# The end stage of an adaLN attention block: casts and dQ matmuls in other places, fp32 gradient tiles from GpSimd, transposes' buffers at 512 B

## The chip, the core and the metric

The kernel runs on one core of a Trainium2 chip. The metric is the device time of one execution in microseconds, the median of several runs. A profile is one further view: one execution, recorded by the hardware profiler. Below, PE is TensorE, DVE is VectorE, ACT is ScalarE, POOL is GpSimd and SP is SyncE, which here only issues DMAs.

## The reference

One transformer block with adaptive layer norm, forward and backward, with S = 2048 tokens, D = 512 features, H = 32 heads of 16, F = 1792 hidden units, all inputs in bf16:

```python
mod = silu(c) @ w_mod            # six rows: sa, ca, ga, sb, cb, gb
h  = layernorm(x) * (1 + ca) + sa
x1 = x + ga * (softmax_attention(h @ wqkv) @ wo)
h2 = layernorm(x1) * (1 + cb) + sb
y  = x1 + gb * (relu(h2 @ w1 + b1)**2 @ w2 + b2)
out, vjp = jax.vjp(block, x, wqkv, wo, w1, b1, w2, b2, c, w_mod)
return (out, *vjp(grad_out))
```

The outputs are y and the gradients of x, wqkv, wo, w1, b1, w2, b2, c and w_mod (`out_0` to `out_9`).

## The kernel before

The work runs in stages. In brackets stands the time of each stage in the profiled run before.

1. **Forward attention with the MLP in its shadow** (0 to 981 us). Queries go in four chunks of 512 tokens. ACT's exponentials (L385) set the pace. Projections, layer norms and the MLP of earlier chunks are background generators that are advanced between the attention's pieces (`bg.step`, `bg.until`, `bg.take`).
2. **The last chunk** (`last_chunk`, L743, about 982 to 1055). The attention's pools are closed, and the last 512 tokens go through the output projection `wo`, the second layer norm, the MLP and its backward. Here `gT` is the transposed slice of `grad_out`, fetched by a transposing DMA from SP (L776). It is the right-hand side of `du_mm` (L794), whose first groups are computed ahead between the four token tiles of the output projection (L800). Each such tile is added to x by DVE (L801, `x1_l`), normalised, and written as `xh`; turns of `xh` on PE (L763) feed the MLP's first layer (L821).
3. **dW1 and dW2** (`gen_dw1`, L927, and `gen_dw2`; about 1055 to 1169). dW1 goes block by block over 14 slices of 128 hidden units. Each slice needs `du_blk`, a transposing DMA from DRAM issued by SP, two slices ahead, and a `w1_blk` from POOL. PE multiplies (L964), and DVE finishes the gradient and two sums over it into a scrap tile `junk`.
4. **The attention's backward** (`attn_bwd`, L1364; about 1169 to 2450). Scores and exponentials are computed again, DVE forms the score gradients `ds` (L1438), and `ds` is needed twice: as it is for dK and dV, and transposed for dQ. Most of the transposing is done by DMAs (`dsT`, L1446, 256 of them, issued by SP), the rest by turns on PE. `dq` (L1412) adds 32 matmuls of a group to the accumulator `accq`; its finished chunk goes by DVE to `dq_t`, the token-major gradient of Q. `dk_t` and `dv_t` are the same for K and V. Crossbar buffers here are the SBUF tiles that the transposing DMAs read or write: `ds`, `dsT`, `du_blk`, `a_blk`, `dqT`, `dq_t`, `dk_t`, `dv_t`.
5. **The tail of the backward and the end stage** (`attn_bwd`'s last lines and `phase6`, L1572; about 2434 to 2567). The gradient of wqkv is a product per part `t` (0 for Q, 1 for K, 2 for V) and row block `kt`: `dw_mm` is 16 matmuls on PE (3.5 us), `dw_end` two steps on ACT and DVE and a store by POOL. Three of these products (`k0`, `v0`, `k1`) and the column sums (`col_sum`, `cs_bc`) start in the backward's tail; the other nine are `dw(t, kt)`.

The end stage is a list of such steps, written out by hand:

- `dx(st)`, for each of 16 token tiles: 12 matmuls over `dqT`, the transposed gradients of Q, K and V (PE, L1638); an eviction by ACT (L1643); the layer norm's backward on DVE (L1654, L1656); `cast(st)`, which writes the tile's fp32 residual gradient as bf16 into `dx1b` (ACT, L1676); ACT adds a term to the fp32 tile `gp` (L1652); a store by POOL.
- `load_a(i)`, for each pair of token tiles, three pairs ahead: three transposing DMAs into `dqT` and two loads of fp32 residual gradients into `dx1_6`, all from SP.
- `dwo(nt)`: 16 matmuls over `dx1b`, one for each token tile (L1681), the gradient of `wo`.
- `mod(j)`, for each of the six rows: one matmul, a copy and four scalings on ACT (L1707) into `dwm7`, a tile with one buffer, a 512 KB store by POOL (L1708), and four dots on DVE.
- `diag`, `dsa`, `load_wmod`, `load_wo`, `load_o`: small steps and loads for the above (the loads from POOL).

Order: PE, SP and, in the backward's core, POOL follow the order of the program; in the backward's tail and in `phase6` all engines do. Elsewhere a scheduler may reorder ACT, DVE and POOL. Tiles are placed in SBUF by pools, one behind the other, so that a tile's start follows from the sizes of those ahead of it.

Of the kernel before, what the change touches and what calls it, by code (L numbers as in the profile page):

```python
# [9 lines left out]
BF16 = mybir.dt.bfloat16  # L10
F32 = mybir.dt.float32
# [8 lines left out]
P = 128  # L20
# [85 lines left out]
class K:  # L106
# [160 lines left out]
    def phase_fwd(self):  # L267
# [9 lines left out]
        self.dgb_acc = pp.tile([P, D], F32, name="dgb_acc")  # L277
        self.csq = pp.tile([P, D], F32, name="csq")
        self.dc_part = pp.tile([P, DT, 6], F32, name="dc_part")
        self.dsb_col = pp.tile([P, DT], F32, name="dsb_col")  # L280
        self.dcb_col = pp.tile([P, DT], F32, name="dcb_col")
        self.db1 = pp.tile([P, FT], F32, name="db1")
# [80 lines left out]
        for n, (qc, g, jp) in list(enumerate(order))[2:]:  # L363
# [36 lines left out]
            if jp == 1 and n + 1 < len(order):  # L400
                if n < 2 * NQ - 1:
                    bg.until(-(g + 1))
                KT = KTn
        bg.until(f"fc2_{SC - 2}")
        x0s = []
        for k in range(2):
            t = self.mk.tile([P, D], BF16, name="x0", bufs=2)
# [335 lines left out]
    def last_chunk(self, bg, O_b, x0s):  # L743
# [27 lines left out]
        g_tm = e0.tile([P, ST, D], BF16, name="g_tm")  # L771
        xh2 = e0.tile([P, ST, D], BF16, name="xh2")
        gt4, xh = g_tm[:, st0:, :], xh2[:, st0:, :]
        OT = mk.tile([P, 4, DT, P], BF16, name="fT", bufs=2)
        gT = mk.tile([P, DT, 512], BF16, name="fT", bufs=2)
        nc.sync.dma_start_transpose(gT[:], io["grad_out"][0, s0:s0 + 512, :])  # L776
        nc.sync.dma_start(gt4, tm_v(io["grad_out"][0]))
        nc.sync.dma_start(xh2[:, :st0, :], self.xhat2_d.rearrange("(st p) d -> p st d", p=P)[:, :st0, :])
        nc.sync.dma_start(g_tm[:, :st0, :], io["grad_out"][0].rearrange("(st p) d -> p st d", p=P)[:, :st0, :])
# [147 lines left out]
    def gen_dw1(self, sb, xh2):  # L927
        nc, io = self.nc, self.io
        D, F, ST, DT, FT = self.D, self.F, self.ST, self.DT, self.FT
        db1 = self.db1  # L930
        w1_v = io["B_w1"].rearrange("(kt p) f -> p kt f", p=P)
        dw1_v = io["out_4"].rearrange("(kt p) f -> p kt f", p=P)
        dcb_part = sb.tile([P, DT, FT], F32, name="dcb_part", bufs=1)
        dsb_part = sb.tile([P, DT, FT], F32, name="dsb_part", bufs=1)
        db1_row = sb.tile([1, F], BF16, name="db1_row", bufs=1)
        nc.vector.memset(dcb_part[:], 0.0)
        nc.vector.memset(dsb_part[:], 0.0)
        blks = []

        def load(ft):  # L940
            r = sb.tile([P, ST, P], BF16, name="du_blk", bufs=3)
            cuts = (0, ST - 4, ST) if ft < 2 else (0, ST)
            for (a, b) in zip(cuts, cuts[1:]):
                nc.sync.dma_start_transpose(r[:, a:b, :], self.duT_d[ft, :, a * P:b * P])
            w = sb.tile([P, DT, P], BF16, name="w1_blk", bufs=3)
            with nc.allow_non_contiguous_dma(reason="256B runs"):
                nc.gpsimd.dma_start(w[:], w1_v[:, :, ft * P:(ft + 1) * P])
            diag = sb.tile([P, P], F32, name="diag", bufs=3)
            nc.gpsimd.tensor_scalar(diag[:], self.ident_f[:], db1[:, ft:ft + 1], 1.0, ALU.mult, ALU.mult)
            blks.append((r, w, diag))  # L950

        for ft in range(2):
            load(ft)
        yield 0
        for ft in range(FT):
            if ft + 2 < FT:
                load(ft + 2)
            else:
                yield ("dw1", 0)
            du, w1_blk, diag = blks[ft]  # L960
            g4 = self.dps.tile([P, DT, P], F32, name="dps")
            for kt in range(DT):
# [12 lines left out]
            for kt in range(DT):  # L975
                nc.scalar.activation(t1[:, kt, :], csb[:], ACT.Copy, scale=self.mod_col(3)[:, kt:kt + 1])
                nc.vector.scalar_tensor_tensor(dw1[:, kt, :], g4[:, kt, :], self.opcbT[:, kt:kt + 1], t1[:, kt, :], ALU.mult, ALU.add)
                junk = sb.tile([P, P], F32, name="junk")
                nc.vector.scalar_tensor_tensor(junk[:], g4[:, kt, :], 1.0, w1_blk[:, kt, :], ALU.mult, ALU.mult,
                                               accum_out=dcb_part[:, kt, ft:ft + 1])  # L980
                junk2 = sb.tile([P, P], F32, name="junk")
                nc.vector.scalar_tensor_tensor(junk2[:], csb[:], 1.0, w1_blk[:, kt, :], ALU.mult, ALU.mult,
                                               accum_out=dsb_part[:, kt, ft:ft + 1])
            with nc.allow_non_contiguous_dma(reason="256B runs"):
                nc.gpsimd.dma_start(dw1_v[:, :, ft * P:(ft + 1) * P], dw1[:])
        nc.gpsimd.dma_start(io["out_5"].rearrange("(o f) -> o f", o=1), db1_row[:])
        nc.vector.tensor_reduce(self.dcb_col[:], dcb_part[:], axis=AX.X, op=ALU.add)
        nc.vector.tensor_reduce(self.dsb_col[:], dsb_part[:], axis=AX.X, op=ALU.add)
# [286 lines left out]
    def phase5(self):  # L1275
# [6 lines left out]
        self.dv_t = opa.tile([P, ST, D], BF16, name="dv_t")  # L1282
        self.opa = opa
        self.junk6 = opa.tile([P, D], F32, name="junk6")
        self.dsa_part = opa.tile([P, DT, 3], F32, name="dsa_part")
        nc.gpsimd.memset(self.dsa_part[:], 0.0)
        nc.gpsimd.memset(self.dc_part[:], 0.0)
        assert ST * self.H == D
# [10 lines left out]
    def open_bwd(self):  # L1299

        nc = self.nc
        S, ST, D, DT = self.S, self.ST, self.D, self.DT
        xp = self.open_pool("p5x", bufs=1, side="right")
        self.wp = self.open_pool("p5w", bufs=1, side="right")
        cp = self.open_pool("p5c", bufs=1, side="right")
# [1 line left out]
        self.q0 = xp.tile([P, 2 * S + 3 * ST * 4 * DH], BF16, name="q0")  # L1307
        self.xhat1_6 = m01[:, :ST * D].rearrange("p (st d) -> p st d", d=D)
        self.wq_6 = self.q0[:, :3 * DT * D].rearrange("p (kt n) -> p kt n", n=3 * D)
        self.kvs = cp.tile([P, 1], F32, name="kvs")  # L1310
        nc.vector.memset(self.kvs[0:64], self.scale)
        nc.vector.memset(self.kvs[64:P], 1.0)
        m23 = cp.tile([P, 4 * S], BF16, name="m23")
# [50 lines left out]
    def attn_bwd(self):  # L1364
# [9 lines left out]
        G = 4  # L1374
# [81 lines left out]
            nc.scalar.copy(dsT[:, 0:4, :], tp[:])  # L1456
            grp.append(dsT)

        tick = kvp.tile([1, 1], BF16, name="tick")
        T = self.T0  # L1460
        turnq, last = [], None
        for g in range(NQ):
# [50 lines left out]
        with tc.manual_schedule(engines=ALL):  # L1513
# [12 lines left out]
            k0, v0, k1 = [dpp.tile([P, 512], F32, name="dp") for _ in range(3)]  # L1526
            self.dw_mm(k0, 1, 0, 0, ST // 2)
            turn(*turnq.pop(0))
            for _ in range(G):
                dq(pendq.pop(0), [0, 1])  # L1530
            self.dw_mm(v0, 2, 0, 0, ST // 2)
            self.dw_mm(k0, 1, 0, ST // 2, ST)
            self.col_sum(1)
            self.dw_mm(v0, 2, 0, ST // 2, ST)
            self.col_sum(2)
            self.cs_bc(1)
            while pendq:
                dq(pendq.pop(0), [0, 1])
            self.cs_bc(2)
            self.dw_mm(k1, 1, 1, 0, ST)  # L1540
        assert not turnq and not pend
        self.dw_open = [(1, 0, k0), (2, 0, v0), (1, 1, k1)]

# [28 lines left out]
    def phase6(self):  # L1572
# [45 lines left out]
        def load_a(i):  # L1618
            s2 = 2 * i
            dqT = wk.tile([P, 3, 2, DT, P], BF16, name="dqT", bufs=3)  # L1620
            for t in (1, 2, 0):
                nc.sync.dma_start_transpose(dqT[:, t].rearrange("p s n k -> p (s n) k"),
                                            parts[t][:, s2:s2 + 2, :].rearrange("p s d -> p (s d)"))
            dx1s = [wk.tile([P, D], F32, name="dx1_6", bufs=6) for _ in range(2)]
            for k in range(2):
                nc.sync.dma_start(dx1s[k][:], dx1_v[:, s2 + k, :])
            nxt[i] = (dqT, dx1s)

        for i in range(2):
# [85 lines left out]
        diag(3, self.dsb_col)  # L1715
        diag(4, self.dcb_col)
        dw(1, 2, stp, "st")
        dsa(1)
        self.col_sum(0)
        load_a(2)  # L1720
        dw(1, 3, dpp, "dp")
        dsa(2)
# [2 lines left out]
        dx1b = sb.tile([P, ST, D], BF16, name="dx1b")  # L1725
        O_tm = sb.tile([P, ST, D], BF16, name="O_tm")
        dga = dgs[2] = sb.tile([P, D], F32, name="dga_acc")
        dx(0)
        dw(2, 1, dpp, "dp")
        mod(3)  # L1730
        dx(1)
        load_wmod(4)
        dw(2, 2, dpp, "dp")
        dx(2)
        load_wmod(0)
        dw(2, 3, dpp, "dp")
        mod(4)
        dx(3)
        load_o(0)
        dw(0, 0, dpp, "dp")  # L1740
        dx(4)
        load_wmod(1)
        dw(0, 1, dpp, "dp")
        load_o(1)
        dsa(0)
        dx(5)
        dw(0, 2, dpp, "dp")
        load_o(2)
        dx(6)
        dw(0, 3, dpp, "dp")  # L1750
        nc.vector.tensor_reduce(dsa_col[:], dsa_part[:], axis=AX.X, op=ALU.add)
        nc.vector.tensor_reduce(dca_col[:], dca_part[:], axis=AX.X, op=ALU.add)
        load_o(3)
        dx(7)
        diag(0, dsa_col)
        diag(1, dca_col)
        load_wo(0)
        load_wo(1)
        dx(8)
        mod(0)  # L1760
        dx(9)
        mod(1)
        dx(10)
        load_wmod(2)
        dx(11)
        for st in range(12, ST):
            cast(st)
        dwo(0)
        dx(12)
        load_wo(2)  # L1770
        dwo(1)
        dx(13)
        load_wo(3)
        dwo(2)
        dwo(3)
        dx(14)
# [83 lines left out]
```

## Time and profile before

| | us |
|---|---|
| median of 5 runs | 2571.58 |
| the five runs | 2568.52, 2571.07, 2571.58, 2574.01, 2574.53 |
| profiled execution, its own time | 2568.52 |
| its span in the profile | 2566.7 |
| PE busy in the span | 2467.2 (96%) |
| ACT busy | 2313.4 (90%) |
| DVE busy | 1762.0 (69%) |
| POOL busy | 559.5 (22%) |
| DMA bytes, mean rate | 432.18 MB, 168 GB/s |

The profiled execution is the fastest of the five runs. Its span is 1.8 us shorter than its time. The mean granted clock of TensorE was 0.994 of full speed. Busy shares are means over the stages named above, which have different limits. In lines of the chain of waits the two numbers are the start and the length of a piece; in lines of the timeline they are the start and the duration of a group of like instructions, and the bracket at the end is the idle time of the engine before it and what ended that. A line number refers to the kernel before.

### The profile page before, as it was taken

How to read it: one execution, taken by the hardware profiler on the slowest of the kernel's cores; microseconds unless marked ns; L12 is line 12 of the kernel's file. 1: busy time of each engine (PE TensorE's matmuls, PEld its weight loads, DVE VectorE, ACT ScalarE, POOL GpSimd, SP SyncE). 2: the span in 40 equal slices, each digit the busy share in tenths (PEclk: the TensorE clock that was granted, in tenths of full speed). 3: DMA queues.
4: the chain of work that ended last, by engine and by line, in shares of the span. 5: the costliest groups of instructions: out<-in, count | busy, mean ns of one | idle time of the engine just before them, and what ended most of it. 6: DMA issues, size and time to landing. Idle time of an engine off the chain costs nothing.

```text
span 2566.7 us, 77585 instructions
## 1 busy us (share of the span) xinstructions
PE 2467.2 (96%) x31011; PEld 1223.9 (48%) x31239; DVE 1762.0 (69%) x3651; ACT 2313.4 (90%) x3761; POOL 559.5 (22%) x1113
## 2 busy tenths in 40 slices
PE   8999899999999998999999999999999999999997
PEld 4555555555555554663444444444444444444443
DVE  6222223423322344667999999999999999999976
ACT  7999999999999996416999999999999999999954
POOL 3454521320221131452111111111111111101122
PEclk9999999999999999999999999999999999999999
DMA  4598752450451154999999999999999999999995
GB/s 165 117 177 199 174 93 86 108 111 22 118 129 49 46 139 117 237 216 207 204 202 201 200 200 201 199 205 199 201 201 200 203 205 198 198 199 203 226 224 157
DMA packets 1196032, 432.18 MB, mean 168 GB/s; under 512 B 1137604, under 2 KB 1163078, under 8 KB 1195670
## 3 DMA queue, kind: packets, MB, share of 16 engines
q1 hardware_dynamic: 1158342, 324.75, 65.4%
q0 software_dynamic: 37328, 102.47, 13.3%
q8 instruction: 244, 4.00, 0.6%
q14 instruction: 118, 0.97, 0.1%
HBM read 74.26 MB, written 68.69 MB: 56 GB/s over the span
## 4 chain that ended last, share of the span: by engine, by line
PE 60%; ACT 28%; DMA 5%; issue 5%; DVE 1%; POOL 0%; SPq 0%; ACTq 0%; POOLq 0%; DVEq 0%
ACT pu L385 24%; PE st L1497 19%; PE acckv L1390 10%; PE accq L1412 8%; PE st L382 4%; PE dp L1436 3%; ACT pu L1501 2%; DMA dsT<-ds 2%; PE st L1455 2%; PE dps L1015 2%; PE accbank L316 2%; PE dps L964 1%; PE dp L1546 1%; PE st L1638 1%; PE pps L1176 1%
## 5 line engine op out<-in xcount | busy, mean ns | idle before, releaser
L1438 DVE TENSOR_TENSOR ds<-dp,pu 128x512 bf16<-128x512 f32 x2048 | 1237.1, 682 | 18.1 <-PE dp L1436 11.1
L1501 ACT ACTIVATE pu<-st 128x512 bf16<-128x512 f32 x2048 | 1074.0, 612 | 77.6 <-PE st L1497 50.8
L385 ACT ACTIVATE pu<-st 128x1024 bf16<-128x1024 f32 x992 | 912.0, 1077 | 5.0 <-PE st L382 4.5
L382 PE MATMUL st<-QTm,KTq 128*128 128x512 bf16 x1859 | 561.6, 377 | 27.0 <-ACT pu L385 6.0
L316 PEld LDWEIGHTS <-pu 128*128 128x128 bf16 x8192 | 347.0, 96 | 236.3 <-issue 3.4
L316 PE MATMUL accbank<-Vaug,pu 128*128 128x17 bf16 x8192 | 357.7, 171 | 8.3 <-ACT Vaug L505 1.1
L1436 PE MATMUL dp<-m,q 64*128 64x512 bf16 x1024 | 345.9, 383 | 4.9 <-DVE ds L1438 4.1
L1436 PE MATMUL dp<-m,dOTg 64*128 64x512 bf16 x1024 | 344.0, 381 | 0.0
L1412 PEld LDWEIGHTS <-dsT 128*128 128x128 bf16 x8192 | 239.8, 96 | 213.8 <-issue 209.2
L1497 PE MATMUL st<-m,q 64*128 64x512 bf16 x1024 | 320.0, 382 | 9.0 <-ACT pu L1501 7.5
L1497 PE MATMUL st<-m,QTg 64*128 64x512 bf16 x1024 | 319.1, 381 | 9.6 <-ACT pu L1501 7.9
L382 PEld LDWEIGHTS <-KTq 128*128 128x128 bf16 x1984 | 188.3, 96 | 177.5 <-issue 125.5
L1485 POOL COPY tick<-ds 1x1 bf16<-1x1 bf16 x215 | 37.9, 176 | 1020.5 <-DVE ds L1438 1020.5
L1456 ACT COPY dsT<-st 128x512 bf16<-128x512 bf16 x256 | 152.5, 596 | 5.1 <-PE st L1455 5.1
L1390 PE MATMUL acckv<-pu,q 128*16 128x512 bf16 x1024 | 154.5, 382 | 0.0
L1390 PE MATMUL acckv<-ds,q 128*16 128x512 bf16 x1024 | 154.4, 382 | 0.0
L1390 PE MATMUL acckv<-pu,dOg 128*16 128x512 bf16 x1024 | 154.0, 381 | 0.0
L1390 PE MATMUL acckv<-ds,Qg 128*16 128x512 bf16 x1024 | 154.0, 381 | 0.0
L1412 PE MATMUL accq<-Kg,dsT 128*128 128x16 bf16 x4096 | 143.5, 170 | 2.4 <-DMA dsT<-ds 2.2
L1412 PE MATMUL accq<-q,dsT 128*128 128x16 bf16 x4096 | 144.0, 170 | 1.6 <-DMA dsT<-ds 1.6
L296 POOL DMA_DIRECT2D QTm<-QTq_d x124 | 63.1, 511 | 336.4 <-PE st L382 315.8
L323 DVE RECIPROCAL rl<-accbank 128x4 f32<-128x4 f32 x128 | 22.9, 179 | 152.8 <-PE accbank L316 152.7
(363 smaller groups left out, 2800.1 us busy)
## 6 DMA issues: line engine op xcount, KB each, us to landing
KTq<-KTq_d POOLq DMA_DIRECT2D x24, 512.0 KB, 3.9
duT_d<-auT POOLq DMA_DIRECT2D x4, 1792.0 KB, 8.8
aT_d<-rT POOLq DMA_DIRECT2D x3, 1792.0 KB, 13.2
KTq_d<-KTq SPq DMA_DIRECT2D x32, 128.0 KB, 2.0
QTq_d<-ev_fm SPq DMA_DIRECT2D x32, 128.0 KB, 2.9
VTq_d<-vT POOLq DMA_DIRECT2D x4, 1024.0 KB, 6.5
O_d<-O POOLq DMA_DIRECT2D x4, 1024.0 KB, 5.6
dsT<-ds SPq DMA_TRANSPOSE x256, 6.6
```

The source lines that it names most:

```text
L296: nc.gpsimd.dma_start(QTm[j][32 * j:32 * j + 32, :], self.QTq_d[g, 32 * j:32 * j + 32, 512 * qc:512 * (qc + 1)])
L316: nc.tensor.matmul(acc[:, a, sub, :], lhsT=pu[:, a, sub * P:(sub + 1) * P], rhs=Vaug[:, kb, h, :], start=(kb == 0 and a == 0 and sub == 0) ...
L382: nc.tensor.matmul(stt[:, a, :], lhsT=KT[:, kb * P:(kb + 1) * P], rhs=QTm[2 * jp + a][:], start=True, stop=True)
L385: nc.scalar.activation(pu[:], stt[:], ACT.Exp, scale=self.scale)
L1015: nc.tensor.matmul(pt[:], lhsT=a[:, st, :], rhs=g_tm[:, st, :], start=(st == 0), stop=(st == ST - 1))
L1390: nc.tensor.matmul(acckv[r:r + DH, :], lhsT=T[n][:, ib, col:col + DH], rhs=src[:, a, :], start=(ib == 0), stop=(ib == ST - 1))
L1412: nc.tensor.matmul(accq[:, ib, a, :], lhsT=dsT[:, (i * 2 + a) * 4 + sub, :], rhs=T["K"][:, 4 * c + sub, col:col + DH], start=(c == 0 and i ...
L1436: nc.tensor.matmul(dp[:], lhsT=T["dOT"][rd, ib * P:(ib + 1) * P], rhs=masked["VT"][2 * jp + a][rd, 512 * c:512 * (c + 1)], start=True, sto ...
L1438: nc.vector.tensor_tensor(dsg[:, i, a], dp[:], pu[:, a, :], ALU.mult)
L1456: nc.scalar.copy(dsT[:, 0:4, :], tp[:])
L1497: nc.tensor.matmul(stt[:], lhsT=T["QT"][rs, q], rhs=masked["KT"][2 * jp + a][rs, c0:c0 + 512], start=True, stop=True)
L1501: nc.scalar.activation(pu[:, a, :], stt[:], ACT.Exp, scale=self.scale)
```

## The change

- `gT` and its neighbour in the ring `fT` are allocated, and the transpose of the last slice of `grad_out` is issued, while the forward attention's pools are still open, ahead of the loads of `x0`, rather than in `last_chunk`.
- `dsa_part`, `tick` and `kvs` move to the persistent pool, and with them the two clearing memsets of `dsa_part` and `dc_part`, which then run near the start of the program. Three small tiles that nothing uses (`pad`, `pad_1`, `pad_r`) and a second buffer less for `junk` shift what is placed behind them: `ds` and `dsT` from 256 B past a multiple of 512 to a multiple of 512, `du_blk` and `a_blk` from 96, `dqT` from 480, `dq_t`, `dk_t` and `dv_t` from 160.
- In the backward's tail the last two groups of dQ matmuls move behind the halves of `k0` and `v0`, the column sums and `k1`; `cs_bc(2)` stands between `k1` and them.
- In `phase6` each `dx` moves behind one `dw`; `cast(12)` and `cast(13)` move to before `dx(10)`, `cast(14)` and `mod(1)` to before `dx(11)`; `col_sum(0)` moves ahead of `dsa(1)`; some POOL loads move by a step.
- The fp32 tiles of pairs 3 to 7 are loaded by POOL, not by SP.

```diff
+        self.dsa_part = pp.tile([P, DT, 3], F32, name="dsa_part")
+        self.tick = pp.tile([1, 1], BF16, name="tick")
+        self.kvs = pp.tile([P, 1], F32, name="kvs")
+        pp.tile([P, 112], BF16, name="pad")
...
         bg.until(f"fc2_{SC - 2}")
+        self.OT_l = self.mk.tile([P, 4, DT, P], BF16, name="fT", bufs=2)
+        self.gT_l = self.mk.tile([P, DT, 512], BF16, name="fT", bufs=2)
+        nc.sync.dma_start_transpose(self.gT_l[:], self.io["grad_out"][0, S - 512:, :])
         x0s = []
...
-        OT = mk.tile([P, 4, DT, P], BF16, name="fT", bufs=2)
-        gT = mk.tile([P, DT, 512], BF16, name="fT", bufs=2)
-        nc.sync.dma_start_transpose(gT[:], io["grad_out"][0, s0:s0 + 512, :])
+        OT, gT = self.OT_l, self.gT_l
...
+        sb.tile([P, 32], BF16, name="pad_1", bufs=1)
...
-                junk = sb.tile([P, P], F32, name="junk")
+                junk = sb.tile([P, P], F32, name="junk", bufs=1)
...
-        self.dsa_part = opa.tile([P, DT, 3], F32, name="dsa_part")
...
+        self.open_pool("pad_r", bufs=1, side="right").tile([P, 240], BF16, name="pad_r")
...
-        self.kvs = cp.tile([P, 1], F32, name="kvs")
...
-        tick = kvp.tile([1, 1], BF16, name="tick")
+        tick = self.tick
...
             turn(*turnq.pop(0))
-            for _ in range(G):
-                dq(pendq.pop(0), [0, 1])
             self.dw_mm(v0, 2, 0, 0, ST // 2)
             self.dw_mm(k0, 1, 0, ST // 2, ST)
             self.col_sum(1)
             self.dw_mm(v0, 2, 0, ST // 2, ST)
             self.col_sum(2)
             self.cs_bc(1)
+            self.dw_mm(k1, 1, 1, 0, ST)
+            self.cs_bc(2)
             while pendq:
                 dq(pendq.pop(0), [0, 1])
-            self.cs_bc(2)
-            self.dw_mm(k1, 1, 1, 0, ST)
...
-                nc.sync.dma_start(dx1s[k][:], dx1_v[:, s2 + k, :])
+                (nc.gpsimd if i > 2 else nc.sync).dma_start(dx1s[k][:], dx1_v[:, s2 + k, :])
...
         dw(1, 2, stp, "st")
+        self.col_sum(0)
         dsa(1)
-        self.col_sum(0)
...
+        dw(2, 1, dpp, "dp")
         dx(0)
-        dw(2, 1, dpp, "dp")
         mod(3)
+        dw(2, 2, dpp, "dp")
         dx(1)
         load_wmod(4)
-        dw(2, 2, dpp, "dp")
...
         mod(0)
         dx(9)
-        mod(1)
+        cast(12)
+        cast(13)
         dx(10)
         load_wmod(2)
+        mod(1)
+        cast(14)
         dx(11)
-        for st in range(12, ST):
-            cast(st)
+        cast(15)
         dwo(0)
```

More of the change, by code (lines that the diff above doesn't have):

```diff
@@ L977, in gen_dw1 @@
                 nc.vector.scalar_tensor_tensor(dw1[:, kt, :], g4[:, kt, :], self.opcbT[:, kt:kt + 1], t1[:, kt, :], ALU.mult, ALU.add)
-                junk = sb.tile([P, P], F32, name="junk")
+                junk = sb.tile([P, P], F32, name="junk", bufs=1)
                 nc.vector.scalar_tensor_tensor(junk[:], g4[:, kt, :], 1.0, w1_blk[:, kt, :], ALU.mult, ALU.mult,
                                                accum_out=dcb_part[:, kt, ft:ft + 1])
-                junk2 = sb.tile([P, P], F32, name="junk")
+                junk2 = sb.tile([P, P], F32, name="junk", bufs=1)
                 nc.vector.scalar_tensor_tensor(junk2[:], csb[:], 1.0, w1_blk[:, kt, :], ALU.mult, ALU.mult,
@@ L1727, in phase6 @@
         dga = dgs[2] = sb.tile([P, D], F32, name="dga_acc")
+        dw(2, 1, dpp, "dp")
         dx(0)
-        dw(2, 1, dpp, "dp")
         mod(3)
+        dw(2, 2, dpp, "dp")
         dx(1)
         load_wmod(4)
-        dw(2, 2, dpp, "dp")
+        dw(2, 3, dpp, "dp")
         dx(2)
         load_wmod(0)
-        dw(2, 3, dpp, "dp")
         mod(4)
+        dw(0, 0, dpp, "dp")
+        load_o(0)
         dx(3)
[L1739 to L1742, printed above, removed]
         dw(0, 1, dpp, "dp")
@@ L1745, in phase6 @@
         dsa(0)
-        dx(5)
+        dx(4)
+        load_wmod(1)
         dw(0, 2, dpp, "dp")
         load_o(2)
-        dx(6)
+        dx(5)
         dw(0, 3, dpp, "dp")
+        load_o(3)
         nc.vector.tensor_reduce(dsa_col[:], dsa_part[:], axis=AX.X, op=ALU.add)
         nc.vector.tensor_reduce(dca_col[:], dca_part[:], axis=AX.X, op=ALU.add)
-        load_o(3)
-        dx(7)
+        dx(6)
         diag(0, dsa_col)
@@ L1758, in phase6 @@
         load_wo(1)
+        dx(7)
         dx(8)
@@ L1771, in phase6 @@
         dwo(1)
+        load_wo(3)
         dx(13)
-        load_wo(3)
         dwo(2)
```

## The prediction

> **What bounds the kernel now.** I read the page first: the engines' shares, the forty slices, the chain. Then, for each place that the change touches, the chain of waits and the timeline there.
>
> ```profile
> span 2566.7 us, 77585 instructions
> ...
> PE 2467.2 (96%) x31011; PEld 1223.9 (48%) x31239; DVE 1762.0 (69%) x3651; ACT 2313.4 (90%) x3761; POOL 559.5 (22%) x1113
> ...
> L1438 DVE TENSOR_TENSOR ds<-dp,pu 128x512 bf16<-128x512 f32 x2048 | 1237.1, 682 | 18.1 <-PE dp L1436 11.1
> ```
>
> The time is 2568.52 us in the profiled run: 2566.7 of span and 1.8 around it. That run is the fastest of the five; the median, 2571.58, lies 3.06 above it. I add up against 2568.52 and then add 3.06. The page says three things. PE is short of work almost nowhere. The attention backward (1175 to 2435) is paced by DVE, whose 2048 score-gradient instructions of L1438 fill 1237 of about 1260 us, so nothing PE saves there is worth more than DVE's few waits. And outside it PE works in program order, so a microsecond of PE's waiting is a microsecond of the kernel if the work behind hangs on PE. The change can therefore gain only where PE idles. The chain shows four such places by name:
>
> ```profile
> 982.68 4.80 DMA O_d<-O
> ...
> 988.61 5.14 DMA fT<-in_grad_out_dram
> 993.75 0.04 issue
> 993.79 1.02 PE dps L794 x4
> ```
> ```profile
> 1055.94 9.05 DMA du_blk<-duT_d
> ...
> 1073.82 12.53 DMA du_blk<-duT_d
> ```
> ```profile
> 1169.97 0.50 POOL m L1486
> 1170.48 4.49 DMA out_dram<-dw
> ```
> ```profile
> 2429.51 9.89 DMA dsT<-ds
> 2439.41 0.05 issue
> 2439.45 0.86 PE accq L1412 x28
> ```
>
> In each the reader is to see a DMA as the piece that PE or DVE waited for. The timeline then gives the idle time itself in its last bracket, with the one place of the end stage where PE waits for ACT:
>
> ```profile
> 993.79 1.02 PE L794 MATMUL dps<-fT,W2gbT 128*128 128x512 bf16 x4 [4.05 <-DMA fT<-in_grad_out_dram]
> 2439.45 0.86 PE L1412 MATMUL accq<-Kg,dsT 128*128 128x16 bf16 x28 [2.22 <-DMA dsT<-ds]
> 2525.65 2.56 ACT L1707 ACTIVATE dwm<-dm,scT 128x512 bf16<-128x512 f32 x4 [2.61 <-DMA out_dram<-dwm]
> 2529.34 0.38 PE L1681 MATMUL gps<-dx1b,O_tm 128*128 128x512 bf16 x1 [3.65 <-ACT dx1b L1676]
> ```
>
> **Part 1, the gradient's transpose asked for early.** SP issues it at 988.61, behind two x loads that wait for the forward's last store (982.68 + 4.80), and it lands at 993.75. In the changed order it stands ahead of those loads, right behind a transpose that SP issued at 966.01. With 3.10 of issue and 5.14 of landing it is there by about 980, and 4.05 us of PE's idle time go. Not all of it arrives: the chain runs on through DVE's L801 for the fourth tile (996.49, idle 3.48 before it), and DVE had other work until 993.01, part of it a wait for POOL's power (0.55). The fourth tile's normalisation, xh, its turns and L821 (1003.54) hang behind. So the shift is 3.5. The bounds are 2.5 (the x0 load for the third tile, issued ahead of the fourth's, lands late) and 4.9: the 4.05 with what the slow clock cost, since the four matmuls of L800 at 994.65 took 1.80 where their like took 1.03, at a granted clock of 0.50 between 996 and 998. A rule of the Trainium skill, page "TensorE: Matmul & The Clock Gate", section "What's actually happening", says that an idle window of some 3.4 us halves PE's clock until it has been busy for another; the trace agrees here, and by the rule the loss ends with the gap. Everything up to the dW1 stage is one chain on PE, so I carry 3.5 to the end.
>
> **Part 2, dW1 stage and the buffers at 512 B.** Small tiles that nothing reads move the transposes' tiles in SBUF: dsT and ds from 256 past a multiple of 512 to a multiple, du_blk and a_blk from 96, dqT from 480, the dQ, dK and dV tiles from 160. No instruction is added. Price: in the trace, the 256-byte packets of transposes take 18 ns in the median at every start I could tell apart (96, 192, 256, 416, 480), so I take nothing. None starts at 0, so that the bound is open to both sides: from the gain if every wait for these transposes went (8.0 us in 5 waits for du_blk, 1.6 for dsT inside the backward) to the loss below. The second junk buffer goes away; DVE waits for itself there, is 60 to 90% busy and is not what PE waits for: 0, plus or minus 0.5. One KTq load moves into POOL's queue in this stage, ahead of w1 loads and dW1 stores that have two blocks of slack (7 us): 0, if that slack is gone 1.
>
> The Trainium skill has a rule that speaks against the alignment, page "DMA: Bandwidth & Descriptors", section "How a descriptor splits into AXI transactions": a start on a multiple of 256 B costs no extra beats. By it dsT gains nothing and only du_blk and dqT could; no packet in this trace is shorter for being aligned.
>
> **Part 3, start of the backward.** POOL's two memsets (1169.47 and 1169.58) move to the program's start and its 0.50 KTq load to part 2's stage. They stood ahead of the last dW2 store (1170.48), whose landing releases DVE's first ds (1175.24, idle 3.88). The store can issue from about 1170.1: 0.4 us, on DVE's path. Bounds 0 and 0.5.
>
> **Part 4, tail of the backward.** PE's two last groups of dQ matmuls, 64 of them, go behind the halves of dK and dV, the column sums and k1. The stall of 2.22 goes, since dsT landed at 2439.4 and they now run near 2448; PE issues the same instructions up to dw(1,2), which started at 2453.67. Gain 2.2. What is later: dQ's eviction by DVE (2449.46) and with it SP's first dqT transposes (2449.56) and the evictions of k0, v0, k1 behind it on DVE, by about 2 us (64 matmuls at 0.96 for 32). Who waits: dx(0), at 2463.38, whose transposes (the last issued at 2452.22, 5.7 to land) are there near 2458 and then near 2460. It has 3 us in hand, and dw(2,1), 3.6 us of PE, now stands ahead of it. Hence 0; without that cover 1.2 of the 2.2 goes back.
>
> **Part 5, the order of the end stage.** Each dx(k) goes behind one dw: PE has no gap from 2453.84 to 2512.7, so exchanging them is worth nothing. The gain can only be at dwo(0), where PE idles 3.65, 1.87 and 1.28. The cause is ACT: it waits 2.61 for mod(0)'s store, then scales for 2.56, and only at 2528.11 evicts dx(10); dx(11) follows at 2530.36 and four casts to 2534.96. In the changed queue dx(10) and its cast, and casts 12 and 13, stand ahead of mod(1)'s scaling, so the 2.61 is filled; but that scaling (0.57 + 2.56) and cast(14) now stand ahead of dx(11)'s eviction. At most 2.61 comes, and one PE gap of dwo(0) stays, with its slow clock behind it. I take a half, 1.2; below, -1.0, if mod(1)'s scaling comes too late for dx(11). Ten fp32 loads go from SP (0.55 each in the median, up to 1.5) to POOL (0.54 for such a load or store, 10 x 0.54 = 5.4 of issue, in a queue that idles 48.0 us for DVE's dx): 0, with the price in a rival.
>
> **Sum.** -3.5 - 0.4 - 2.2 - 1.2 = -7.3: 2568.52 - 7.3 = 2561.2, and with 3.06 for the median 2564.3. With the bounds of the parts (-4.9 - 0.5 - 2.2 - 2.6 = -10.2, and -2.5 - 0 - 1.0 + 1.0 = -2.5) 2561.4 to 2569.1. A measurement of this kernel tells 0.2%, 5.1 us, from no change.
>
> **Rivals.** *Swallowed in dW1.* If the du_blk transposes are paced by something that does not move with PE, part 1's 3.5 turns into longer waits for du_blk: -3.8, 2567.8, the same. For it: 8.0 us of waits, SP issuing a du_blk every 4.4 us with DMA at 1.1. Against it: the first of them waits for a turn's eviction on ACT (1055.51) that PE's chain releases, so the stage starts earlier whole. One in ten.
>
> *Alignment pays.* Half of the 9.6 us of waits for these transposes goes: -7.3 - 4.8, 2559.5. For it: these waits are the largest left. Against it: 18 ns at each start. 0.16.
>
> *Alignment costs, and SP becomes the bound: slower.* The backward issues 256 dsT transposes between 1180.3 and 2435.5, one each 4.90 us, and an issue keeps SP for 3.62 (median; 3.39 to 5.93). SP has 1.28 to spare. If a multiple of 512 puts all 128 partitions' rows to the same place at a time and the issue grows past 4.90, SP paces DVE, and each 0.05 costs 256 x 0.05 = 12.8. At 4.95: 12.8 - 7.3 = +5.5, 2577.1. For it: some issues already take 5.9 and none starts at a multiple of 512, so no row excludes it. Against it: it needs a third more. 0.14, with smaller costs of that kind.
>
> *GpSimd's loads come late.* The last pair's fp32 tiles are asked for behind dx(9)'s store, which ended at 2524.3; two issues and 4.3 to 5.6 of landing make 2529.7 to 2531, and cast(14) in front of dx(11)'s eviction would hold ACT some 4 us: -3.3, 2568.3, the same. By the Trainium skill, page "SBUF — State Buffer", on the trap of DVE blocking DMA, GpSimd's descriptors wait while DVE holds the shared port; the 0.54 per issue beside a busy DVE does not show it. 0.05.
>
> **How the numbers follow.** My forecast has 0.55: 0.42 of it faster, 0.13 within 0.2%. Faster: 0.42 + 0.16 = 0.58. Same: 0.13 + 0.10 + 0.05 = 0.28. Slower: 0.14. The likeliest case's own range is 2561.4 to 2569.1; for 8 in 10 it reaches down to 2556 (most of the aligned gain) and up to 2576 (the start of the slower case).
>
> **What would show it.** Right: L794's first group without a DMA wait and L821 near 1000; first ds near 1174.8 less that shift; L1412's last 64 without a stall; dwo(0) with under 5 us of gaps. Wrong: du_blk waits longer by part 1's gain; dsT issues or landings other than 3.6 and 6.6; DVE's idle time on L1438 other than 18; ACT waiting for a dx1 load before cast(12) or cast(14).

## The result and the profile after

The change makes the kernel slower by a third of a per cent, where 0.3% faster was predicted.

| | us |
|---|---|
| before, median of 80 runs | 2573.80 (2562.21 to 2592.98) |
| after, median of 43 runs | 2581.82 (2567.17 to 2600.47) |
| ratio after to before | 1.0033, 95% interval 1.0023 to 1.0043: +8.5 us (5.9 to 11.1) |
| profiled execution after: time, span | 2572.91, 2571.1 |

The page of the changed kernel, the same lines as were shown of before:

```profile
span 2571.1 us, 77574 instructions
...
PE 2466.4 (96%) x31011; PEld 1223.8 (48%) x31239; DVE 1764.3 (69%) x3651; ACT 2312.5 (90%) x3761; POOL 566.1 (22%) x1123
...
L1443 DVE TENSOR_TENSOR ds<-dp,pu 128x512 bf16<-128x512 f32 x2048 | 1237.5, 682 | 18.4 <-PE dp L1441 10.1
```

The work is the same, and so is the attention backward: from the first `ds` to the last it took 1258.5 us (1169.7 to 2428.2) after 1258.4. The differences lie ahead of it and behind it. Timeline of the changed kernel, the groups that answer to those of before (start, duration, group, idle time before it):

```profile
988.44 1.03 PE L799 MATMUL dps<-fT,W2gbT 128*128 128x512 bf16 x4
997.61 2.76 PE L826 MATMUL pps<-fT,w 128*128 128x512 bf16 x12 [0.52 <-DVE fT L771]
1169.74 6.23 DVE L1443 TENSOR_TENSOR ds<-dp,pu 128x512 bf16<-128x512 f32 x10 [4.48 <-DMA out_dram<-dw]
2445.86 3.61 PE L1549 MATMUL st<-dk_t,m 128*128 128x512 bf16 x15
2521.59 0.75 DVE L1659 SCALAR_TENSOR_TENSOR dx<-t,rstd,dx 128x512 bf16<-128x512 f32 x1 [5.74 <-DMA out_dram<-dx]
2529.07 0.58 PE L1684 MATMUL gps<-dx1b,O_tm 128*128 128x512 bf16 x1 [7.57 <-ACT dx1b L1679]
2537.03 2.29 PE L1684 MATMUL gps<-dx1b,O_tm 128*128 128x512 bf16 x5 [7.37 <-ACT dx1b L1679]
```

In the first four lines the work comes earlier. The groups of L799 have no wait; the MLP's first layer starts at 997.61 (1003.54 before), the first `ds` at 1169.74 (1175.24), and dw(1,2) at 2445.86 (2453.67): the end stage began 7.8 us early. Some 1.2 of this is a difference of the two executions (the last forward exponential at 978.9 and 980.1). The last three lines are where it was lost, and more: from dw(1,2) to the end of the span it took 125.2 us after 113.0. dwo(0) waits twice, 7.57 and 7.37 us, for casts on ACT; ACT waits for DVE; and DVE's last step of a `dx` waits for the *store* of the `dx` two tiles back, since its tile has two buffers. The waits from 2440 on, first of before, then of after (engine and line, what was waited for: sum in us, times, longest):

```profile
PE gps L1681 <- ACT dx1b L1676: 5.5, 2, 3.7
ACT dwm L1707 <- DMA out_dram<-dwm: 2.8, 2, 2.6
DVE junk L1566 <- DMA wmod<-in_w_mod_dram: 1.5, 1, 1.5
```
```profile
PE gps L1684 <- ACT dx1b L1679: 14.9, 2, 7.6
DVE dx L1659 <- DMA out_dram<-dx: 11.2, 4, 5.7
DVE junk L1569 <- DMA wmod<-in_w_mod_dram: 6.5, 1, 6.5
ACT dwm L1710 <- DMA out_dram<-dwm: 4.2, 2, 2.2
```

DVE's 11.2 us for dx stores do not stand in the profile of before. All of these are transfers that GpSimd asks for. The dx stores landed after 5.1 us in the median and 10.8 at most (3.2 and 4.3 in the profile of before), the loads of the attention output (`O_tm`) after 10.6 in the median (4.7). Such a pair of profiles does not show that the change did this: in a second profile of the kernel before (e16 below) the dx stores took 4.4 and up to 15.1 us, `O_tm` 13.0, and DVE waited 4.1 us for dx stores. What GpSimd's loads do is read from all profiles, behind e16.

The other place is the dW1 stage, where PE's idle time changed its cause ("issue" is time in which PE waited for nothing that the profile shows). The view of the stage's matmuls, before and after (us, times):

```profile
  DMA du_blk<-duT_d: 8.0, 5
  issue: 0.7, 1
```
```profile
  issue: 4.7, 4
  DVE junk L985: 3.8, 3
  DMA du_blk<-duT_d: 0.2, 1
```

PE waits for DVE there now. The stage took 61.8 us after 61.7, though it had lost its waits for `du_blk`.

### The profile page after: what moved, and what is told of

It is laid out like the page before. It is cut to its first block, busy times and chain, and to the rows that moved or that the text cites. A ratio compares the mean times of both kernels' runs of the same rounds, so it can differ in the third digit from the quotient of the medians.

```text
span 2571.1 us, 77574 instructions
## 1 busy us (share of the span) xinstructions
PE 2466.4 (96%) x31011; PEld 1223.8 (48%) x31239; DVE 1764.3 (69%) x3651; ACT 2312.5 (90%) x3761; POOL 566.1 (22%) x1123
## 4 chain that ended last, share of the span: by engine, by line
PE 58%; ACT 30%; issue 5%; DMA 4%; DVE 2%; POOL 1%; ACTq 0%; DVEq 0%; POOLq 0%
ACT pu L389 26%; PE st L1502 19%; PE acckv L1395 10%; PE accq L1417 8%; PE st L386 4%; PE dp L1441 3%; ACT pu L1506 2%; PE st L1460 2%; PE dps L1021 2%; PE accbank L320 2%; DMA dsT<-ds 1%; PE dps L970 1%; PE pps L1182 1%; DMA fT<-xh 1%; DMA out_dram<-dwm 1%
```

## The experiments

Theories: **Q**, GpSimd's fp32 loads fill its queue and make its stores late; **O**, the new order itself; **X**, the starts at 512 B slow transfers; **D**, the end stage is paced by the DMA engines, so that what PE gains is waited for; later **J**, the single junk buffer. Each ratio is to the kernel before, run beside it on the same chip; microseconds are the ratio times 2572.

| run | what it has of the change | ratio, 95% interval | us |
|---|---|---|---|
| (after) | all | 1.0033, 1.0023 to 1.0043 | +8.5 |
| e1_sp_loads | all but GpSimd's loads | 1.0012, 0.9994 to 1.0029 | +3.1 |
| e2_pool_loads | GpSimd's loads | 1.0003, 0.9981 to 1.0026 | +0.8 |
| e3_order | order of the end stage | 0.9998, 0.9980 to 1.0016 | -0.5 |
| e4_front | gT, tail, allocations | 1.0016, 0.9994 to 1.0037 | +4.1 |
| e5_alloc | allocations | 1.0017, 1.0000 to 1.0035 | +4.4 |
| e6_no_alloc | all but allocations | 1.0009, 0.9991 to 1.0026 | +2.3 |
| e7_gt | early gT | 0.9988, 0.9970 to 1.0006 | -3.1 |
| e8_tail | later dQ matmuls | 1.0011, 0.9992 to 1.0029 | +2.8 |
| e9_alloc_junk2 | allocations, two junk buffers | 1.0008, 0.9991 to 1.0025 | +2.1 |
| e10_junk1 | one junk buffer | 1.0020, 1.0003 to 1.0036 | +5.1 |
| e11_cut | none; 3.5 MB of transfers left out | 0.9989, 0.9977 to 1.0002 | -2.8 |
| e12_cut_moves | gT, tail, order; 3.5 MB left out | 0.9937, 0.9916 to 0.9958 | -16.2 |
| e13_moves | gT, tail, order | 0.9961, 0.9940 to 0.9982 | -10.0 |
| e14_after_junk2 | all, two junk buffers | 1.0016, 0.9987 to 1.0044 | +4.1 |
| e15_mod_late | e13, one mod step later | 0.9957, 0.9937 to 0.9977 | -11.1 |
| e16_before_again | none | 0.9989, 0.9962 to 1.0016 | -2.8 |
| e17_moves_pads | e13, padding, two junk buffers | 1.0001, 0.9976 to 1.0026 | +0.3 |
| e18_moves_junk1 | e13, one junk buffer | 0.9989, 0.9975 to 1.0003 | -2.8 |

**e1, e2: who asks for the loads.** e1 takes the line back in the changed kernel, e2 sets it in the kernel before.

```diff
-                (nc.gpsimd if i > 2 else nc.sync).dma_start(dx1s[k][:], dx1_v[:, s2 + k, :])
+                nc.sync.dma_start(dx1s[k][:], dx1_v[:, s2 + k, :])
```

> The changed kernel with one line undone: the fp32 loads of pairs 3 to 7 are issued by SP again. In the profile of the changed kernel the work up to dw(1,2) came 7.8 us earlier than before, and the end stage then took 12 us longer. Theory Q (the loads fill GpSimd's DMA queue, so that the stores of dx, which DVE's double-buffered tile waits for, and of mod, which ACT's single tile waits for, land late: median 5.1 and 6.1 us after 3.2 and 4.6): about 8 us faster than before, waits of DVE's last dx step for a dx store near 0 (11.2 in the changed kernel), dx stores landing in 3 to 4 us. Theory O (the new order itself does it: mod and dw come earlier, and meet loads that have not landed): no better than the changed kernel, about +8 us against before. Theory X (the aligned buffers make the dqT transposes slow and these hold the DMA engines): like O.

> The kernel before with that one line alone changed: fp32 loads of pairs 3 to 7 issued by GpSimd. Theory Q: 5 to 12 us slower than before, with DVE's last dx step waiting for dx stores and the first dwo group waiting for casts by more than 6.8 us. Theories O and X: within 2 us of before.

Measured: +3.1 and +0.8, which fits neither Q nor O. Q's 8 us are not there, and in e1's profile DVE still waited 6.3 us for one dx store, where Q expected next to nothing. Of the 8.5 of the change 5.4 go with the line (to within 5.2), but in the order of before the line costs nothing that the interval shows.

**e3, e4: order alone, and all but the end stage.** e3 has the list from dw(1,2) to the second dwo as in the diff of the change, nothing else; e4 has that list and the loads as before, and all the rest changed.

> The kernel before with the new order of the end stage alone (from dw(1,2) to the first two dwo), loads on SP. Theory O: 6 to 12 us slower than before, DVE waiting some 6 us for the w_mod load of mod(4). Theories Q and X: within 2 us of before, by the prediction 1.2 faster, with a dwo(0) that still waits about 5 us.

> The changed kernel with the end stage's old order and SP's loads: what stays is the early gradient transpose, the early memsets, the padding and the tail of the backward. Theories Q and O: 6 to 8 us faster than before (the 7.8 of the profile, of which about 1 is a difference between runs in the forward part). Theory X: about as slow as before or slower, with dqT transposes issued in more than the 1.2 to 2.1 us of before.

Measured: -0.5 and +4.1. The order alone is not the cost: O's 6 to 12 lie outside the interval (-5.1 to 4.1). e4 should have been 6 to 8 faster by Q and O. It is not, so that something in the front or the allocations costs some 10 if that gain is there. Its profile had an end stage of 147.0 us from the last `ds` to the end, with the old order (133.1 before); e16 below has 145.2 without any edit, so the 147.0 shows nothing.

**e5 to e8: the parts one by one.** e5 has the allocation lines of the diff alone; e6 all but these; e7 and e8 one edit each.

```diff
 # e7
...
+        nc.sync.dma_start_transpose(self.gT_l[:], self.io["grad_out"][0, S - 512:, :])
...
 # e8
...
+            self.dw_mm(k1, 1, 1, 0, ST)
+            self.cs_bc(2)
             while pendq:
                 dq(pendq.pop(0), [0, 1])
```

> The kernel before with the change's allocations alone: the padding, one junk buffer, dsa_part, tick and kvs in the persistent pool (so also the two memsets early); orders and issuing engines as before. Theory X (the buffers at a multiple of 512 B slow the transposes of du_blk and dqT, or what runs beside them): 5 to 10 us slower. Theory D (the end stage and the dW1 stage are paced by the DMA engines, whose share is 1.0 to 1.2 in both, and the starts of the tiles do not matter): within 2 us of before.

> The changed kernel with the allocations of before: early gradient transpose, dQ matmuls later, new order of the end stage, GpSimd's loads; buffers where they were. Theory X: 4 to 8 us faster than before. Theory D: the same as before or up to 8 us slower (the changed kernel's +8.5), since what PE gains is waited for at DMAs.

> The kernel before with the gradient's transpose issued early, and nothing else. By the prediction's part 1 3.5 us faster, if what follows is a chain on PE. Theory D: 0 to 2 us faster in the time, with the gain in the profile up to L821 (PE idle 4.05 gone) and given back in the dW1 stage as longer waits for du_blk.

> The kernel before with the last dQ matmuls behind the blocks of dK and dV, and nothing else. By the prediction's part 4 2.2 us faster. Theory D: 0 to 3 us slower, since the end stage's transposes start later (they wait for the last dQ) while PE is early, and the end stage waits for them.

Measured: +4.4, +2.3, -3.1, +2.8. The early transpose is near the predicted 3.5, but not told from 0 (7.7 faster to 1.5 slower); the allocations, priced at 0, cost 4.4 (0.0 to 9.0). e6 is not the 4 to 8 faster of X. That the tail's edit, which saves PE 2.2 us, does not make the kernel faster (2.1 faster to 7.5 slower) would fit D.

**e9, e10: which allocation.** e10 is the kernel before with this edit alone (`junk2`, three lines below, has it too); e9 is e5 without it.

```diff
-                junk = sb.tile([P, P], F32, name="junk")
+                junk = sb.tile([P, P], F32, name="junk", bufs=1)
```

> The allocations of the change as in the run e5_alloc, but with two junk buffers as before: du_blk, a_blk, dsT and dqT still start at a multiple of 512 B. In nine profiles the dW1 stage took 62 to 69 us in the four kernels with the new allocations (mean 66.5) and 57 to 64 in the others (mean 60.6). Theory J (the single junk buffer lets the scheduler put POOL's w1 loads and DVE's steps in another order, and PE waits for DVE to free its accumulators): the dW1 stage is back at 57 to 64, and the time within 2 us of before. Theory X (the starts of the tiles): the stage stays at 62 to 69 and the time some 4 us above before.

> The kernel before with the single junk buffer alone; no tile of the transposes moves against 512 B. Theory J: 3 to 6 us slower than before, dW1 stage 62 to 69 us with PE waiting for DVE there by some 5. Theory X: within 2 us of before, stage 57 to 64.

Measured: +2.1, not told from 0, and +5.1 (0.8 to 9.3): theory J. The idle time of the dW1 stage's matmuls, of e10 and then of e9:

```profile
  issue: 9.2, 4
  DVE junk L979: 6.5, 3
  DMA du_blk<-duT_d: 3.8, 4
```
```profile
  DMA du_blk<-duT_d: 3.6, 5
  issue: 0.5, 1
```

From its first matmul to the start of its last, the dW1 stage took 61.8 to 68.9 us in the six kernels with one junk buffer (mean 67.1) and 56.9 to 64.3 in the fourteen profiles with two (mean 60.1). With one, the scheduler also puts DVE's steps and POOL's w1 loads, diagonals and stores of this stage in another order. In e10's trace DVE's order is `dw` (L977), the dot over `csb` (L982), the dot over PE's result (L979); in that of before, L979 stands right behind L977. L979 is what PE waits for, 6.5 us in e10; its 9.2 under "issue" are not explained, and no run has the one order without the other.

**e11, e12: fewer transfers.** Four of six w_mod loads and three of four `O_tm` loads are left out, first in the kernel before, then with the three moves.

```diff
         def load_wmod(j):
+            if j not in (5, 3):
+                wmods[j] = wmods[5]
+                return
...
         def load_o(i):
+            if i:
+                return
...
```

> The kernel before with less to move in the end stage: four of the six w_mod loads and three of the four loads of the attention output are left out (3.5 MB; the products then use the tiles already there, so that dWo, dc and what hangs on them are other numbers). By the packets of before, 896 of 4096 B at 0.204 us over 16 engines, this takes 11 us from the 95 us of DMA work in the end stage. Theory D (the DMA engines pace the end stage): 5 to 11 us faster, with less scatter between runs. If PE and ACT pace it, as the prediction had it: within 2 us of before.

> The same cut, and with it the change's moves: early gradient transpose, later dQ matmuls, new order of the end stage; old allocations, loads by SP. Theory D: with the DMA engines off the path PE's gains show, and this is faster than e11_cut by most of the predicted 3.5 + 2.2 + 1.2 = 6.9 us, at least 4. If the moves are worth nothing for another reason: within 2 us of e11_cut.

Measured: -2.8 and -16.2. The cut alone brings less than D's 5 to 11 in the median, and is not told from 0 (5.9 faster to 0.5 slower). But its twelve runs lie between 2565.1 and 2572.1, 7 us apart; the twelve of e9 and of e10 beside them lie 18.1 and 16.1 apart, the 29 of before 22.8. Much of the scatter goes with these transfers. The moves then bring 13.4 us (to within 6.3; e12 has six runs), twice their predicted 6.9. A summary by stretch, from the last `ds` to the end of the span, of before, e11 and e12 (us; PE, weight loads, DVE, ACT and POOL busy; clock, DMA share, GB/s):

```profile
2433.60:2566.70 133.10, 114.31 (x618) 51.27 (x623) 88.03 (x223) 65.50 (x132) 30.99 (x51) 0.95 0.78 193
```
```profile
2433.20:2566.10 132.90, 114.09 (x618) 51.25 (x623) 88.00 (x223) 65.48 (x132) 25.75 (x44) 0.95 0.69 166
```
```profile
2424.30:2552.60 128.30, 113.87 (x618) 51.69 (x623) 87.76 (x223) 65.38 (x132) 25.84 (x44) 0.96 0.71 172
```

**e13 to e16.** e13 is e6 with the loads by SP; e14 the changed kernel with two junk buffers; e16 the kernel before; e15 is e13 with this:

```diff
         dx(4)
-        load_wmod(1)
...
         dx(10)
-        load_wmod(2)
-        mod(1)
         cast(14)
         dx(11)
         cast(15)
+        load_wmod(1)
         dwo(0)
         dx(12)
         load_wo(2)
         dwo(1)
         load_wo(3)
+        mod(1)
         dx(13)
+        load_wmod(2)
         dwo(2)
```

> The change's three moves (early gradient transpose, later dQ matmuls, new order of the end stage) with the allocations of before and the loads by SP. If GpSimd's loads cost in their own right: 4 to 8 us faster than the run e6_no_alloc, so some 3 to 6 below before. If the end stage is paced by its transfers whoever asks for them: within 2 us of before, as the sum of the single runs has it (-3.1 + 2.8 - 0.5).

> The changed kernel with two junk buffers as before, all else as changed. By e10_junk1 (+5.1 us for one buffer) 4 to 6 us faster than the changed kernel, that is 2 to 5 above before, dW1 stage 57 to 64 us. If the starts at 512 B cost as well: no better than 6 above before.

> As e13_moves, but the step for row 1 of the modulation (its 512 KB load, four dots, 512 KB store) goes from ahead of the first dwo to behind the second, and the load for row 2 with it: nothing is left out, 1.5 MB move from the stretch in which the DMA engines are full (share 1.0 to 1.2) to the last 25 us, where the share is 0.2. Theory D: the first dwo comes earlier, 4 to 8 us faster than e13_moves. If transfers are not what holds the first dwo: no faster, or 2 to 3 slower, since DVE and ACT get 3 us of work more in the last 25.

> The kernel before once more, for a second profile of it. The first profiled execution took 2568.5, the median of 80 runs is 2573.8. If the scatter sits in the transfers: the second profile differs from the first by some us in the dW1 stage (61.7) and from the last ds to the end (133.1), and by under 0.5 in the attention backward between (1258.4).

Measured: -10.0, +4.1, -11.1, -2.8 (this the same code, inside its interval). The three moves alone, with SP's loads and the old allocations, take 2564.11 us in the median. Against e6 that is 12.3 faster (to within 7.0): in the new order GpSimd's loads do cost time. Two more pairs differ by this line alone in the new order, the changed kernel against e1 (5.4, to within 5.2) and e14 against e17 (3.9, to within 9.8); the three weighted together give 7.2 (to within 3.8). e14 is 4.4 below the changed kernel (to within 7.8), which fits one buffer's cost and shows nothing by itself. D does not hold as it was put: e13 should have been within 2 us of before, and e15 4 to 8 faster than e13. e15 is not told from e13 (1.0 faster, to within 7.5); its runs lie 13 us apart, those of e13 22. Its median, 2561.60, is the lowest of the versions that leave nothing out.

e16 settles a point of reading. Its profile by the same stretch, from the last `ds` on, and that of e13, of the changed kernel and of e14:

```profile
2434.40:2579.60 145.20, 120.21 (x627) 52.47 (x623) 87.96 (x223) 65.67 (x132) 30.99 (x51) 0.90 0.84 177
```
```profile
2431.40:2569.10 137.70, 116.61 (x627) 52.07 (x623) 87.47 (x223) 65.39 (x132) 31.16 (x51) 0.93 0.80 187
```
```profile
2428.20:2571.10 142.90, 116.08 (x618) 51.93 (x623) 87.52 (x223) 64.82 (x132) 36.40 (x61) 0.91 0.80 179
```
```profile
2427.50:2580.70 153.20, 118.96 (x627) 52.38 (x623) 87.38 (x223) 64.84 (x132) 36.51 (x61) 0.91 0.88 167
```

The same code, with the same 25.7 MB (length times GB/s), took 133.1 in one execution and 145.2 in the other, while the backward took 1258.4 in both. Length times share is the time that the packets took, over 16 engines: 91 us in e12, 92 in e11, 104 in before, 110 in e13, 114 in after, 122 in e16, 135 in e14. The stage's length follows this number in order (partly because the length is a factor of it; e11 and e12 are the two in which the transfers themselves were changed).

What GpSimd's loads do shows when all profiles with the new order are laid side by side. In the three with GpSimd's loads (after, e6, e14) DVE waits 6.5 to 10.0 us for the w_mod load of `mod(4)` and 11.2 to 17.3 for dx stores; in the six with SP's and nothing left out (e1, e3, e13, e15, e17, e18) 2.4 to 3.7 and 1.3 to 9.4. That w_mod load now stands right behind the two fp32 loads of pair 3. After it was asked for, it takes 8.5 to 12.0 us until DVE starts on it, against 5.7 to 6.8 with SP's loads. First the changed kernel, then e13 (asked for by POOL, used by DVE):

```profile
2476.53 1.07 POOL L1629 DMA_DIRECT2D dx<-dx_d  x2
2477.60 0.76 POOL L1668 DMA_DIRECT2D wmod<-in_w_mod_dram  x1
2486.11 0.69 DVE L1569 SCALAR_TENSOR_TENSOR junk<-dm,wmod 128x512 f32<-128x512 f32 x1 [6.50 <-DMA wmod<-in_w_mod_dram]
```
```profile
2478.36 0.76 POOL L1664 DMA_DIRECT2D wmod<-in_w_mod_dram  x1
2484.90 0.69 DVE L1565 SCALAR_TENSOR_TENSOR junk<-dm,wmod 128x512 f32<-128x512 f32 x1 [3.46 <-DMA wmod<-in_w_mod_dram]
```

So Q holds in the new order, for the w_mod load as for the stores; whether because they share a queue or because the fp32 loads now run beside it was not tried. With the old order nothing parts the two: e2 has 7.7 us of waits for dx stores, the kernels with SP's loads and full transfers 0 to 8.7.

**e17, e18: what takes the moves' gain in e1.**

> e13_moves with the change's padding and persistent tiles (du_blk, a_blk, dsT, dqT start at a multiple of 512 B), but two junk buffers. Theory J (the junk buffer alone costs): as e13_moves, 8 to 12 us faster than before. Theory X (the starts, or what else the allocations move, cost): 4 us or more slower than e13_moves.

> e13_moves with the single junk buffer and no padding. Theory J: 5 to 9 us slower than e13_moves, so 1 to 5 faster than before, with a dW1 stage of 62 to 69 us. Theory X: as e13_moves.

Measured: +0.3 and -2.8. The junk buffer costs the moves 7.2 us (to within 6.5), as J expects. The padding with two junk buffers costs them 10.3 (to within 8.4), against J, though without the moves it cost 2.1 (to within 4.4). e17's own profile, 2558.6 of span, has none of it. That stays open; e13 may also have been measured on the fast side, since the fit below gives the three moves 4.7 us together, not 10.0.

To put all runs together I fitted the sixteen ratios of the kernels with full transfers (without e15, which has an order of its own) to a sum of six terms, each ratio weighted by its interval: early gT -4.3 (to within 3.8), tail +1.5 (3.8), order -1.9 (3.3), junk buffer +3.5 (2.5), the other allocations +3.3 (2.5), GpSimd's loads +5.8 (2.8). The sum is +7.9 against +8.5 measured, which is itself in the fit. What the sum leaves over is no more than the intervals explain (chi squared 11.9 for 10 degrees of freedom); kernels measured together share their runs of before, which the fit does not count. That the loads cost more in the new order, as the pairs of runs and the waits have it, is neither shown nor excluded by the fit.

## Why the prediction was wrong

- **Part 1** was right in the trace: the wait is gone, L821 came 5.9 us earlier, 4.8 of it beyond the difference of the two executions, near the upper bound of 4.9. The time alone does not show it (e7 -3.1, from 7.7 faster to 1.5 slower); in the fit it is 4.3 (to within 3.8). The gain was carried to the dW1 stage and to the first `ds`, and the rival "swallowed in dW1" is not seen (e7's stage: 56.9).
- **Part 2 failed in a term set to 0.** That DVE "is not what PE waits for: 0, plus or minus 0.5" was true of before and was taken for true of after. With one buffer PE waits for DVE; the term is +5.1 by itself (0.8 to 9.3), 2.3 to 7.2 in the four other pairs that differ by it, +3.5 in the fit. The order of the changed kernel's instructions showed that DVE's and POOL's steps were exchanged there; I priced the exchange at nothing because no instruction was added.
- **The starts at 512 B** were priced at 0, and the packets bear it out: in the changed kernel the transposes' 256-byte packets take 18 ns in the median, as at the other starts, dsT lands after 6.8 us in the median (6.6 before), is issued in 3.63 (3.62), and the backward has its old length. The mechanism of neither rival on alignment shows in the traces. The rule of the Trainium skill in "DMA: Bandwidth & Descriptors", "How a descriptor splits into AXI transactions", says the same for dsT, and the trace agrees. The +3.3 of the fit for padding and early memsets has no place in the profiles that I could find; it is not in the dW1 stage, which took 57.7 to 58.7 us in the three profiles with these starts and two buffers.
- **Part 3** failed, at small cost: the store left POOL 0.29 us after DVE wrote it (0.39 before), and landed after 5.18 rather than 4.49, so DVE waited 4.48, not 3.88. The two memsets had run beside DVE's work.
- **Part 4**: from the last `ds` to dw(1,2) it took 17.7 us after 20.1: 2.4, predicted 2.2. That later transposes cost nothing since dx(0) has 3 us in hand held for dx(0), which waits for none. The gain is not seen in the time (e8 +2.8, fit +1.5), and why is open. The first transpose was issued 17.9 us after the last `ds`, 16.0 before, ahead of a stretch in which the DMA share is above 1. That this eats the gain is argued, not shown: e8's profile has one wait of 2.8 us for a transpose of `dqT`, and the second profile of before, without the edit, one of 7.5.
- **Part 5, the loads, is the step that failed most.** "0, with the price in a rival": it is +5.8 in the fit (to within 2.8), and 12.3, 5.4 and 3.9 in the three pairs with the new order. The rival had the wrong victim. It let the fp32 loads come late for cast(14), and in the changed kernel no cast waits for such a load. Late came what GpSimd asks for behind them: the w_mod load, and with the dx stores DVE's two-buffered `dx` tile and, through DVE, ACT's casts. I had written that POOL idles 48.0 us and that the loads take 5.4 of issue. That is the price on POOL as an engine; the queue of transfers it feeds was not priced.
- **Part 5, the order**, forecast at 1.2, is not told from 0: 0.5 faster in e3, 1.9 in the fit (to within 3.3). dwo(0) waits 7.5 us for casts in e3's profile and 14.9 in the changed kernel's, where gaps of under 5 were to show that the forecast was right.
- **The base.** I said PE has no gap from 2453.84 to 2512.7 and took the end stage for paced by PE. PE is indeed without a gap there in both profiles of before. But the DMA share is 1.0 to 1.2 in it, and I used that number only for the dW1 stage: in the second profile the transfers were still behind at 2520, and PE waited 7.5 us for one. And the first profile was of a short execution: 133.1 us from the last `ds` on, 145.2 in the second. Adding 3.06 for "the median" moved the total, but not the waits, which were read as if they were those of every run.

The three moves alone were 3.5 + 2.2 + 1.2 = 6.9 us in the working. e13 measured 10.0 (4.6 to 15.4), but five other pairs that differ by the moves alone run from 13.4 faster (e12 against e11) to 1.5 slower (e6 against e2); the six weighted together give 6.4 (to within 2.6), the fit 4.7. So the size of that sum is borne out; its terms one by one are not.

## What to carry to other kernels

Price a moved transfer by what stands behind it in its new queue, and follow each store to the tile whose next writer waits for it. Where the DMA share is at 1, transfers can fall behind though PE shows no gap there: in the second profile of before PE was busy for all of 2480 to 2500, at a share of 1.11, and then waited 7.5 us for one transpose. A buffer count is an edit of the order wherever a scheduler decides it; compare the orders of the engines there, and do not carry a "not what PE waits for" from before to after. Where runs lie 1% apart, take a second profile of the kernel before to see which stage the scatter is in, before reading waits of 2 us off the first.

## What the runs showed of the hardware

The packets of the same 25.7 MB in the same code took 104 us of the 16 DMA engines' time in one execution and 122 in the other (0.78 x 133.1 and 0.84 x 145.2). The share can pass 1: it was 1.16 from 2460 to 2480 in the first profile of before. With 3.5 MB less, twelve runs lay 7 us apart. What makes packets longer in some executions is not settled by these runs. The Trainium skill says in "DMA: Bandwidth & Descriptors", "Issuing engines are not separate DMA queues", that transfers of all issuing engines share the same 16 DMA engines and that asking from another engine saves only the sequencer's time. The runs agree that nothing is won, and add a cost: 12.3, 5.4 and 3.9 us in the three pairs with the new order (to within 7.0, 5.2 and 9.8), 0.8 with the old one (to within 5.8).
